# First unit of an attention kernel: row turns one slot later, modulation ahead of the first turn, second x tile loaded early

## The chip, the cores and the metric

The kernel runs on one core of a Trainium2 chip. Its time is device microseconds of a whole run; the span in a profile is from the first to the last instruction of one profiled run. The engines are named as in the profile: PE is TensorE (PEld its weight loads), DVE VectorE, ACT ScalarE, POOL GpSimd, SP the engine that issues most loads. All times inside a run are microseconds from the start of its span.

## The reference, cut to what matters

```python
mod = silu(c) @ w_mod                      # six rows of 512: sa, ca, ga, sb, cb, gb
h = layernorm(x) * (1 + ca) + sa           # x: 2048 x 512
q = h @ wq                                 # 32 heads of 128; k, v caches: 8 groups, 2048 keys
p = softmax(q k^T / sqrt(128));  o = p v
x = x + ga * (o @ wo)
# then a gated MLP over the same rows, with a 2048 x 2048 spatial product
```

The argument concerns only the first 35 us: how the first four row tiles (128 rows each) of `x` become queries while the first scores are already being computed.

## The kernel before

A *unit* is one group of four heads and one row tile; it has eight *slots*. Slot i of unit u computes scores for 256 keys (`qk`, two matmuls of 512 columns, then one exponential of 1024 columns on ScalarE), and the values (`pv`) of unit u - 1. `fill` is work put at the end of a slot, `at` work put at its start. `bank2()` gives one of two score buffers `s_ps`, `bank("misc")` one of two other PSUM banks. TensorE executes its matmuls in exactly this program order. A *turn* transposes the normalised rows of one row tile on TensorE and then scales and shifts them by `ca` and `sa` (four *modulations* on VectorE). The *projection* makes queries of the turned tile. `warm(n)` is n idle matmuls on zeros. `mod_part` computes the columns of `sa` or `ca` with 16 matmuls of one column; where the text says "the modulation" in one word, it means the second such set, `ca`.

```python
# loads, all on SP (cut): w_mod first and second half, wq in two parts, then
load_k_nat(0)
load_k_nat(1)
nc.sync.dma_start(out=x_sb[:, 1:CT, :], in_=x_dram[:, 1:CT, :])     # row tiles 1 to 3
# (x tile 0 comes on the ScalarE queue)
...
xns0 = ln1_norm(0, 1, ln1_stats(0, 1))
mc_ps = bank("misc")
warm(10)
mod_part(0, wmod_a, 0, mc_ps)          # 16 matmuls of one column: sa
warm(6)
x_ps = [...]
for dt in range(NDT):                  # first turn: transpose row tile 0
    nc.tensor.transpose(x_ps[dt % 2][...], xns0[0][...], ident[:])
mod_part(1, wmod_a, D, mc_ps)          # 16 matmuls: ca
mod_copy(0, mc_ps)
warm(2)
...                                    # modulate, project tile 0, first scores
def first_norm():                      # at the end of slot 0
    k_turn((4, 5, 6, 7), (nc.vector.tensor_copy,))
    ln_stats(mv1, 2, x_sb[:, 2, :])
    first["x1"] = ln1_norm(1, 1, first["r1"])
    ln_stats(mv1, 3, x_sb[:, 3, :])
    first["r2"] = rstd_of(mv1[:, 2:4, :], 2, "ln1")

def first_turn():
    ln1_turn(1, 1, first["x1"])        # 4 transposes, then 4 modulations on VectorE
    first["x2"] = ln1_norm(2, 2, first["r2"])

at(0, 2, first_turn)
at(0, 5, lambda: ln1_turn(2, 2, first["x2"]))
fill[0, 0] = [first_norm]
for i in (1, 2, 4):
    fill[0, i] = [lambda: warm(1)]     # one idle matmul
fill[0, 3] = qproj(0, list(range(REP)), P, P)                 # 16 matmuls, tile 1
rest_q = qproj(0, [0, 1], 2 * P, 2 * P) + qproj(0, [2, 3], 2 * P, 2 * P)
fill[0, 6], fill[0, 7], fill[1, 0] = rest_q[0:5], rest_q[5:11], rest_q[11:16]
```

`ln1_turn` puts its four blocks into two banks, two blocks in each:

```python
for half in range(2):
    t_ps = bank("misc")[:].bitcast(BF16).rearrange("p (k q) -> p k q", k=2)
    ...                                # transposes of blocks 2*half, 2*half+1, then their modulation
```

Of the kernel before, what the change touches and what calls it, by code (L numbers as in the profile page):

```python
# [15 lines left out]
P = 128  # L16
# [559 lines left out]
def kernel(  # L576
# [19 lines left out]
    nc = tc.nc  # L596
    _, S, D = A_x.shape
    _, HKV, SK, DH = A_k_cache.shape
    HQ = A_wq.shape[1] // DH
    REP = HQ // HKV  # L600
# [9 lines left out]
    CT = 512 // P  # L610
# [7 lines left out]
    x_dram = A_x[0].rearrange("(t p) d -> p t d", p=P)  # L618
# [27 lines left out]
    x_sb = res.tile([P, NT, D], BF16, name="x_sb")  # L646
# [9 lines left out]
    wmod_a = res.tile([P, NDT, 2 * D], BF16, name="wmod_a")  # L656
# [6 lines left out]
    def bank(name):  # L663
        return psum.tile([P, 512], FP32, name=name)

    def bank2():
        return psum.tile([P, 1024], FP32, name="s_ps")
# [35 lines left out]
    def load_k_nat(half):  # L703
        t0, t1 = half * NKT // 4, (half + 1) * NKT // 4
        nc.sync.dma_start(
            out=k_nat[:, t0 * P : t1 * P].rearrange("p (t d) -> p t d", d=DH),
            in_=k_rows[:, t0:t1, :],
        )
# [35 lines left out]
    for dts in (slice(0, 2), slice(2, 4)):  # L744
        nc.sync.dma_start(out=wqs[0][:, dts, :], in_=wq_dram[:, dts, 0 : REP * DH])  # L745
    load_k_nat(0)
    load_k_nat(1)
    nc.sync.dma_start(out=x_sb[:, 1:CT, :], in_=x_dram[:, 1:CT, :])

    kT0 = early.tile([P, SK], BF16, name="kT")  # L750
    groups[0] = dict(kT=kT0)
# [23 lines left out]
    def warm(n):  # L775

        w_ps = bank("o_ps")
        for k in range(n):
            nc.tensor.matmul(
                w_ps[:].rearrange("p (r d) -> p r d", r=REP),  # L780
                lhsT=zeros[:, 0, :],
                rhs=zeros[:],
                start=True,
                stop=True,
            )


    def ln1_stats(j0, n):
        for j in range(j0, j0 + n):
            ln_stats(mv1, j, x_sb[:, j, :])  # L790
        return rstd_of(mv1[:, j0 : j0 + n, :], n, "ln1")
# [9 lines left out]
    def hT_of(ch):  # L801
        if ch not in hTs:
            hTs[ch] = res.tile([P, NDT, 512], BF16, name="hT", bufs=NCH)
        return hTs[ch]

    def ln1_mod(dst, src, dt):
        nc.vector.tensor_scalar(
            out=dst,
            in0=src,
            scalar1=modc[:, NDT + dt : NDT + dt + 1],  # L810
            scalar2=modc[:, dt : dt + 1],
            op0=ALU.mult,
            op1=ALU.add,
        )

    def ln1_turn(j0, n, xns):

        ch, c0 = j0 // CT, (j0 % CT) * P
        hT = hT_of(ch)
        for half in range(2):  # L820
            t_ps = bank("misc")[:].bitcast(BF16).rearrange("p (k q) -> p k q", k=2)
            for k in range(2):
                dt = half * 2 + k
                for jj in range(n):
                    nc.tensor.transpose(
                        t_ps[:, k, jj * P : (jj + 1) * P],
                        xns[jj][:, dt * P : (dt + 1) * P],
                        ident[:],
                    )
            for k in range(2):  # L830
                dt = half * 2 + k
                dst, src = hT[:, dt, c0 : c0 + n * P], t_ps[:, k, 0 : n * P]
                ln1_mod(dst, src, dt)
# [10 lines left out]
    def mod_part(i, wmod, w0, mc_ps):  # L844

        for dt in range(NDT):
            for kt in range(NDT):
                nc.tensor.matmul(
                    mc_ps[:, i * NDT + dt : i * NDT + dt + 1],
                    lhsT=wmod[:, kt, w0 + dt * P : w0 + (dt + 1) * P],  # L850
                    rhs=sc_bf[:, kt : kt + 1],
                    start=(kt == 0),
                    stop=(kt == NDT - 1),
                )

    def mod_copy(first, mc_ps):
        c0 = first * NDT
        nc.vector.tensor_copy(out=modc[:, c0 : c0 + NDT], in_=mc_ps[:, 0:NDT])
        nc.vector.tensor_scalar_add(
            out=modc[:, c0 + NDT : c0 + 2 * NDT], in0=mc_ps[:, NDT : 2 * NDT], scalar1=1.0  # L860
        )
# [15 lines left out]
    mc_ps = bank("misc")  # L877
    warm(10)
    mod_part(0, wmod_a, 0, mc_ps)
    warm(6)  # L880

    x_ps = [bank("misc")[:].bitcast(BF16), bank2()[:, 0:512].bitcast(BF16)]
    for dt in range(NDT):
# [2 lines left out]
            xns0[0][:, dt * P : (dt + 1) * P],  # L886
            ident[:],
        )
    mod_part(1, wmod_a, D, mc_ps)
    mod_copy(0, mc_ps)  # L890
    warm(2)
    hT_of(0)
    for k in range(2):
        for dt in (2 * k, 2 * k + 1):
# [3 lines left out]
            else:  # L898
                nc.scalar.activation(
                    out=dst,  # L900
                    in_=src,
# [17 lines left out]
    for hf, copy in enumerate((nc.vector.tensor_copy, nc.scalar.copy)):  # L919
        copy(  # L920
            out=qTs[0][:, 2 * hf : 2 * hf + 2, 0:P],
            in_=q_ps[hf][:, 0 : 2 * P].rearrange("p (h q) -> p h q", h=2),
# [3 lines left out]
    def qproj(b, heads, c0, n):  # L926

        g, ch = divmod(b, NCH)
        if b not in qTs:
            qTs[b] = early.tile([P, REP, 512], BF16, name="qT")  # L930
        one = n * len(heads) <= 512
        ps = {}

        def mm(hh, dt):
            if dt == 0 and (not one or hh == heads[0]):
                ps[0] = bank("misc")
            o0 = (hh - heads[0]) * n if one else 0
            nc.tensor.matmul(  # L938
                ps[0][:, o0 : o0 + n],
                lhsT=wqs[g][:, dt, hh * DH : (hh + 1) * DH],  # L940
                rhs=hTs[ch][:, dt, c0 : c0 + n],
                start=(dt == 0),
                stop=(dt == NDT - 1),
            )
            if dt == NDT - 1 and (not one or hh == heads[-1]):
                hs = heads if one else [hh]
                dst = qTs[b][:, hs[0] : hs[-1] + 1, c0 : c0 + n]
                src = ps[0][:, 0 : len(hs) * n].rearrange("p (h q) -> p h q", q=n)
                nc.vector.tensor_copy(out=dst, in_=src)  # L949

        return [lambda hh=hh, dt=dt: mm(hh, dt) for hh in heads for dt in range(NDT)]

    first = dict(r1=ln1_stats(1, 1))
# [6 lines left out]
    def at(it, slot, fn):  # L960
        later.setdefault((it, slot), []).append(fn)
# [156 lines left out]
    fill = {}  # L1118
# [8 lines left out]
        ln1_turn(1, 1, first["x1"])  # L1127
        first["x2"] = ln1_norm(2, 2, first["r2"])

    at(0, 2, first_turn)  # L1130
    at(0, 5, lambda: ln1_turn(2, 2, first["x2"]))
    fill[0, 0] = [first_norm]
    for i in (1, 2, 4):
        fill[0, i] = [lambda: warm(1)]
    fill[0, 3] = qproj(0, list(range(REP)), P, P)
    rest_q = qproj(0, [0, 1], 2 * P, 2 * P) + qproj(0, [2, 3], 2 * P, 2 * P)
    fill[0, 6], fill[0, 7], fill[1, 0] = rest_q[0:5], rest_q[5:11], rest_q[11:16]

    def ln1_at(ch, stats, norm, turn):
        st = {}  # L1140
# [169 lines left out]
    for f in range(NFT):  # L1310
# [6 lines left out]
        out=ok1[:], in0=rall[:], scalar1=1.0 / SAFE, scalar2=None, op0=ALU.is_ge  # L1317
# [8 lines left out]
        out=bad[:], in0=okm[:], scalar1=-1.0, scalar2=1.0, op0=ALU.mult, op1=ALU.add  # L1326
# [137 lines left out]
```

## Time and profile before

| | before |
|---|---|
| median of six runs | 1323.25 us (1322.82 to 1323.65) |
| span of the profiled run | 1321.5 us |
| first score matmul | 10.63 |
| slot 2's scores of unit 0 | 13.38 |
| slot 2's scores of unit 1 | 21.94 |
| fifth reciprocal of the values (unit 2) | 40.91 |

The prediction shows the lines that carry the argument; to them belong two lines of TensorE's timeline around the first turn, and one of unit 1. The columns of a timeline are start, duration, engine, line, operation, output and inputs, shapes, count, and in brackets the idle time before it and who ended it.

```profile
7.27 0.22 PE L884 MATMUL s_ps<-ident,xn 128*128 128x128 bf16 x1
7.45 0.55 PE L848 MATMUL misc<-sc_bf,wmod_a 128*128 128x1 bf16 x16
...
21.94 0.59 PE L971 MATMUL s_ps<-qT,kT 128*128 128x512 bf16 x2
```

The last block of the first turn runs at 7.27 and the second set of modulation matmuls behind it, as soon as its weights have landed (7.4).

### The profile page before, as it was taken

To read this page: it belongs to the slowest core of one execution; us is meant where nothing else is said; L and a number is where in the kernel's file an instruction comes from. 1 tells how busy PE (TensorE), PEld (TensorE's weight loads), DVE (VectorE), ACT (ScalarE), POOL (GpSimd) and SP (SyncE) were. 2 spreads that over 40 slices of the span, in tenths; PEclk is the share of its full clock that TensorE was granted. 3 is DMA by queue.
4 is the path that set the end of the run, shared out by engine and by line. 5 is a ranking of instruction groups with operands and counts; after the bars stand their busy time and mean duration, and the time that the engine had idled before them with its cause. 6 is when DMAs were issued, how large, how long until landed. Compare 5 with 4: busy or idle time off the path is not lost.

```text
span 1321.5 us, 27879 instructions
## 1 busy us (share of the span) xinstructions
PE 1312.4 (99%) x12335; PEld 858.3 (65%) x12335; DVE 473.5 (36%) x1166; ACT 1077.8 (82%) x1061; POOL 49.4 (4%) x92
## 2 busy tenths in 40 slices
PE   9999999999999999999999999999999999999998
PEld 5666666666666666666666666666666666644445
DVE  5632222222222222222222222222222566794444
ACT  6898999999999999999999999999999999650000
POOL 1200000000000000000000000000000000120000
PEclk9999999999999999999999999999999999999999
DMA  7541022102111112111110211021101111143300
GB/s 180 141 104 33 14 49 37 37 15 51 31 23 35 32 37 37 31 35 37 33 36 14 53 37 33 18 53 21 33 14 21 25 33 30 33 116 80 69 21 26
DMA packets 148704, 58.12 MB, mean 44 GB/s; under 512 B 138368, under 2 KB 144768, under 8 KB 148576
## 3 DMA queue, kind: packets, MB, share of 16 engines
q1 hardware_dynamic: 141776, 37.65, 15.1%
q0 software_dynamic: 4208, 16.39, 4.1%
q10 hardware_dynamic: 2592, 2.23, 0.5%
q8 instruction: 98, 1.61, 0.5%
q14 instruction: 30, 0.25, 0.1%
HBM read 21.37 MB, written 2.10 MB: 18 GB/s over the span
## 4 chain that ended last, share of the span: by engine, by line
PE 98%; DMA 0%; DVE 0%; SPq 0%; issue 0%
PE o_ps L993 35%; PE s_ps L971 33%; PE misc L1025 8%; PE misc L938 8%; PE misc L1344 7%; PE s_ps L1190 2%; PE s_ps L1229 2%; PE o_ps L1365 1%; PE s_ps L1365 1%; DMA x_sb<-in_A_x_dram 0%; PE misc L1101 0%; DVE tmp L1377 0%; DVE yout L1378 0%; DVE bnst L691 0%; SPq L700 0%; SPq L745 0%
## 5 line engine op out<-in xcount | busy, mean ns | idle before, releaser
L978 ACT ACTIVATE pT<-s_ps 128x1024 bf16<-128x1024 f32 x1024 | 1044.5, 1025 | 82.9 <-PE s_ps L971 9.0
L993 PEld LDWEIGHTS <-pT 128*128 128x128 bf16 x8192 | 548.5, 98 | 241.2
L993 PE MATMUL o_ps<-v,pT 128*128 128x129 bf16 x8192 | 631.4, 220 | 0.0
L971 PE MATMUL s_ps<-qT,kT 128*128 128x512 bf16 x2048 | 609.0, 379 | 0.0
L1004 DVE RECIPROCAL rall<-o_ps 128x2 f32<-128x2 f32 x256 | 43.7, 171 | 743.8 <-PE o_ps L993 743.5
L971 PEld LDWEIGHTS <-kT 128*128 128x128 bf16 x2048 | 199.3, 98 | 118.7 <-DVE qT L920 0.5
L1025 PE MATMUL misc<-wo_g,oT 128*128 128x512 bf16 x512 | 194.0, 379 | 0.0
L938 PE MATMUL misc<-hT,wq_g 128*128 128x512 bf16 (+2 forms) x528 | 189.6, 371 | 0.0
L1005 DVE TENSOR_TENSOR onorm<-o_ps,rall 128x256 bf16<-128x256 f32 x256 | 108.7, 425 | 9.0 <-DVE rall L1004 0.3
L1344 PE MATMUL misc<-wsp,z 128*128 128x512 bf16 (+2 forms) x560 | 100.7, 336 | 0.0
L949 DVE CAST qT<-misc 128x512 bf16<-128x512 f32 x127 | 86.3, 681 | 1.8 <-PE misc L938 1.6
L1344 PEld LDWEIGHTS <-z 128*128 128x128 bf16 x560 | 50.6, 98 | 48.5
L1038 DVE TENSOR_TENSOR xacc<-misc,xacc 128x512 f32<-128x512 f32 x112 | 76.2, 680 | 0.0
L938 PEld LDWEIGHTS <-wq_g 128*128 128x128 bf16 x528 | 50.6, 98 | 1.1 <-issue 0.2
L1025 PEld LDWEIGHTS <-oT 128*128 128x128 bf16 x512 | 50.1, 98 | 0.8
L1359 DVE TENSOR_TENSOR gb<-misc,bsp_bc 128x512 bf16<-128x512 f32 (+1 forms) x28 | 18.4, 659 | 59.0 <-PE misc L1344 59.0
L1190 PE MATMUL s_ps<-win_sb,hT 128*128 128x448 bf16 x128 | 27.0, 352 | 0.0
L1200 ACT ACTIVATE z<-s_ps 128x896 bf16<-128x896 f32 x16 | 14.7, 917 | 14.9 <-PE s_ps L1190 14.9
L1229 PE MATMUL s_ps<-hT,win_sb 128*128 128x512 bf16 x112 | 24.5, 379 | 0.0
L1237 ACT ACTIVATE z1T<-s_ps 128x1024 bf16<-128x1024 f32 x14 | 14.3, 1024 | 10.0 <-PE s_ps L1229 9.1
L691 DVE BATCH_NORM_STATS2 bnst<-x_sb 128x6 f32<-128x512 bf16 x32 | 21.9, 684 | 1.5 <-DMA x_sb<-in_A_x_dram 1.0
L715 POOL DMA_DIRECT2D wq_g<-in_A_wq_dram x7 | 5.3, 753 | 420.9 <-PE misc L938 420.9
(87 smaller groups left out, 283.2 us busy)
## 6 DMA issues: line engine op xcount, KB each, us to landing
wq_g<-in_A_wq_dram POOLq DMA_DIRECT2D x7, 512.0 KB, 3.8
v<-in_A_v_cache_dram POOLq DMA_DIRECT2D x7, 512.0 KB, 7.2
wo_g<-in_A_wo_dram POOLq DMA_DIRECT2D x7, 512.0 KB, 4.7
oT<-onorm SPq DMA_TRANSPOSE x128, 2.4
wsp<-in_w_mod_dram POOLq DMA_DIRECT2D x1, 2048.0 KB, 11.7
out_dram<-yout ACTq DMA_DIRECT2D x16, 128.0 KB, 1.7
win_sb<-in_B_w_in_dram POOLq DMA_DIRECT2D x1, 1792.0 KB, 7.7
x_sb<-in_A_x_dram SPq DMA_DIRECT2D x3, 512.0 KB, 5.6
```

The costliest lines, as they stand in the source:

```text
L938: nc.tensor.matmul(ps[0][:, o0 : o0 + n], lhsT=wqs[g][:, dt, hh * DH : (hh + 1) * DH], rhs=hTs[ch][:, dt, c0 : c0 + n], start=(dt == 0), s ...
L949: nc.vector.tensor_copy(out=dst, in_=src)
L971: nc.tensor.matmul(s_ps[:, h * 512 : (h + 1) * 512].rearrange("p (r q) -> p r q", r=REP), lhsT=groups[g]["kT"][:, kt * P : (kt + 1) * P], ...
L978: nc.scalar.activation(out=pTs[u][:, 2 * i : 2 * i + 2, :], in_=s_ps[:].rearrange("p (k q) -> p k q", k=2), func=ACT.Exp, scale=inv_sqrt_dh,)
L993: nc.tensor.matmul(o_ps[:, hh % 2, 0 : DH + 1], lhsT=pTs[u][:, kt, hh * P : (hh + 1) * P], rhs=groups[g]["v1"][:, kt, 0 : DH + 1], start=( ...
L1004: nc.vector.reciprocal(out=rall[:, c0 : c0 + 2], in_=o_ps[:, :, DH])
L1005: nc.vector.tensor_tensor(out=onorms[u][:, hh - 1 : hh + 1, :], in0=o_ps[:, :, 0:DH], in1=rall[:, c0 : c0 + 2].unsqueeze(2).to_broadcast([ ...
L1025: nc.tensor.matmul(X_ps[:], lhsT=oTs[u][:, hh, :], rhs=groups[g]["wo"][:, hh, :], start=(hh == 0), stop=(hh == REP - 1),)
L1038: nc.vector.tensor_tensor(out=xaccs[j][:], in0=X_ps[:], in1=xaccs[j][:], op=ALU.add)
L1190: nc.tensor.matmul(ps[0][:, hf * 512 : hf * 512 + FC], lhsT=h2Ts[j // CT][:, dt, (j % CT) * P : (j % CT + 1) * P], rhs=win_sb[:, dt, FH + ...
L1229: nc.tensor.matmul(ps[0][:, k * 512 : (k + 1) * 512], lhsT=win_sb[:, dt, f * P : (f + 1) * P], rhs=h2Ts[2 * ch2 + k][:, dt, :], start=(dt ...
L1344: nc.tensor.matmul(g_ps[:, :n], lhsT=z2[:, st, f * P : (f + 1) * P], rhs=wsp[t][:, st, c0 : c0 + n], start=(st == 0), stop=(st == NT - 1 a ...
```

## The change

Its intent: take the wait for the second tile's normalised rows out of TensorE's queue by putting the turn behind one more slot of scores, and bring forward what the first turns need.

```diff
     load_k_nat(0)
+    nc.sync.dma_start(out=x_sb[:, 1, :], in_=x_dram[:, 1, :])
     load_k_nat(1)
-    nc.sync.dma_start(out=x_sb[:, 1:CT, :], in_=x_dram[:, 1:CT, :])
+    nc.sync.dma_start(out=x_sb[:, 2:CT, :], in_=x_dram[:, 2:CT, :])
 ...
     warm(6)
+    mod_part(1, wmod_a, D, mc_ps)
 ...                                    # first turn
-    mod_part(1, wmod_a, D, mc_ps)
     mod_copy(0, mc_ps)
 ...
-    at(0, 2, first_turn)
-    at(0, 5, lambda: ln1_turn(2, 2, first["x2"]))
+    at(0, 3, first_turn)
+    at(0, 6, lambda: ln1_turn(2, 2, first["x2"]))
     fill[0, 0] = [first_norm]
-    for i in (1, 2, 4):
+    for i in (1, 2, 3):
         fill[0, i] = [lambda: warm(1)]
-    fill[0, 3] = qproj(0, list(range(REP)), P, P)
+    fill[0, 4] = qproj(0, list(range(REP)), P, P)
 ...
-    fill[0, 6], fill[0, 7], fill[1, 0] = rest_q[0:5], rest_q[5:11], rest_q[11:16]
+    fill[0, 7], fill[1, 0], fill[1, 1] = rest_q[0:5], rest_q[5:11], rest_q[11:16]
```

As in the prediction, the modulation's new place is (a), the load (b), the later slots (c).

## The prediction

> **What bounds the kernel now.** I read the page first: its chain of waits, then its groups.
>
> ```profile
> PE 98%; DMA 0%; DVE 0%; SPq 0%; issue 0%
> L978 ACT ACTIVATE pT<-s_ps 128x1024 bf16<-128x1024 f32 x1024 | 1044.5, 1025 | 82.9 <-PE s_ps L971 9.0
> ```
>
> The chain that ended last is TensorE for 98% of 1321.5 us. ScalarE's exponentials fill 1044.5 us and wait only 9.0 us for scores. So only a microsecond that TensorE idles, or is held back by the exponentials, can be won. Next I read who waited for whom, TensorE alone, whole span; it is the whole list:
>
> ```profile
> PE o_ps L779 <- DVE onorm L761: 1.2, 1, 1.2
> PE misc L825 <- DVE xn L680: 1.1, 1, 1.1
> PE misc L848 <- DMA wmod_a<-in_w_mod_dram: 0.4, 1, 0.4
> PE misc L912 <- DVE hT L807: 0.3, 1, 0.3
> PE s_ps L1365 <- DVE yT L1360: 0.3, 1, 0.3
> ```
>
> These waits sum to 3.3 us, 0.25% of the span. The second is the change's target. The timeline of the first 26 us, one engine at a time, shows it:
>
> ```profile
> 11.71 0.38 PE L779 MATMUL o_ps<-onorm 128*128 128x512 bf16 x1
> 13.15 0.40 PE L825 MATMUL misc<-ident,xn 128*128 128x128 bf16 x4 [1.05 <-DVE xn L680]
> 13.38 0.59 PE L971 MATMUL s_ps<-qT,kT 128*128 128x512 bf16 x2
> ...
> 14.46 1.37 PE L938 MATMUL misc<-hT,wq_g 128*128 128x128 bf16 x16
> ...
> 12.70 0.39 DVE L680 TENSOR_SCALAR xn<-x_sb,mv,rstd_ln 128x512 bf16<-128x512 bf16 x1
> 13.01 0.69 DVE L691 BATCH_NORM_STATS2 bnst<-x_sb 128x6 f32<-128x512 bf16 x1
> 13.73 0.18 DVE L692 BATCH_NORM_AGGREGATE mv<-bnst 128x2 f32<-128x6 f32 x1
> 13.83 1.07 DVE L807 TENSOR_SCALAR hT<-misc,modc 128x128 bf16<-128x128 bf16 x4
> ...
> 11.26 1.94 ACT L978 ACTIVATE pT<-s_ps 128x1024 bf16<-128x1024 f32 x2 [0.68 <-PE s_ps L971]
> 14.01 1.94 ACT L978 ACTIVATE pT<-s_ps 128x1024 bf16<-128x1024 f32 x2 [0.81 <-PE s_ps L971]
> 16.30 4.98 ACT L978 ACTIVATE pT<-s_ps 128x1024 bf16<-128x1024 f32 x5 [0.35 <-PE s_ps L971]
> ```
>
> The reader is to see three things. The turn of the second row tile (L825) stands in program order ahead of slot 2's scores, and its normalised rows exist only at 13.09, so the queue stands still behind it. ScalarE then starves 0.81 us. And the projection of that tile (L938, 14.46) waits inside itself for the four modulations on VectorE, which end at 14.90.
>
> **What the Trainium skill says.** "TensorE: Matmul & The Clock Gate", Part 2, Step-by-step: only weight loads are pulled ahead; "The MATMULs themselves stay in program order". The trace agrees: slot 2's scores need nothing from the turn, yet run 0.23 us after it, at 13.38. The same page, Part 1, puts 512 columns at about 216 ns back to back; the chain lists pairs of score matmuls at 0.43 us. "DMA: Bandwidth & Descriptors", Anatomy of one DMA, says of the software path that a fixed part of some 2 us is mostly the receipt of the last write; these loads are of the hardware path. Of it the trace shows that landings trail the bytes: by the GB/s of 1 us windows some 1.18 MB (the first x tile and both modulation halves) had moved by 6.1 us, while the second half landed at 1.48 + 5.9 = 7.38.
>
> **The change part by part.** No instruction is added or removed except one more DMA issue; the warming matmuls stay three (slots 1, 2, 3 in place of 1, 2, 4).
>
> (a) Modulation columns ahead of the first turn: 16 small matmuls, 7.45 to about 7.86. They can't start before 7.38, where their weights land; today the four transposes (7.09) run in that gap. Afterwards TensorE waits some 0.3 us, then does the columns, then transposes at 7.87 to 8.1. The column copies on VectorE keep 8.04 to 8.27 and the first modulation 8.30; it needs a transpose done by about 8.1. The query projection begins at 8.79, and its weight load was put down to a DMA:
>
> ```profile
> PEld L912 <- DMA wq_g<-in_A_wq_dram: 0.8, 1, 0.8
> ```
>
> The second half of these weights lands at 2.76 + 6.0 = 8.76. So this part is worth 0, within 0.1 either way.
>
> (b) The second x tile ahead of the second part of k. Its statistics started at 10.75, having waited 0.23 us for the 384 KB load (4.35 + 6.4 = 10.75). Alone it is 128 KB, and at the 370 GB/s of 8 to 9 us lands some 0.7 us ahead of the other two tiles and 0.4 ahead of where the k part was: about 9.7. VectorE is free at 10.52 after its copy of the first queries, so the statistics start 0.2 earlier. But the k copy behind them still waits for TensorE's transposes (11.06 plus 0.39), and the next tile's statistics follow it, so normalised rows come only 0.08 earlier, at about 13.0. The second k part lands at 3.87 + 5.8 + 0.4, about 10.1, against a need at 11.06: hidden. The transposing load of the other half of k moves by up to 0.5 to about 12.2, against slot 4 (15.67): hidden.
>
> (c) Turns and projections one slot later. I re-ran the queue by hand with the durations above: scores 0.43 a slot, a warming matmul 0.21, turn 0.22 (four), projection of the second tile 0.0685 a matmul (13 in 0.89), later projections 0.109 a matmul, values 0.45 a slot; exponentials 1.02 long at a pitch of 0.92 (11.26 to 12.18). Scores of slot n wait for exponential n-2, as s_ps has two buffers.
>
> - Slot 2 scores: exponential 0 ends 12.28, so 12.30 to 12.73, against 13.38.
> - A warming matmul to 12.94; turn waits for rows, 13.07 to 13.29.
> - Slot 3 scores to 13.72, warming to 13.93; slot 4 scores wait for exponential 2 (13.10 to 14.12): 14.14 to 14.57. Before, slot 4 came only after the projection, at 15.84.
> - Projection: three matmuls, then the fourth modulation (now 14.82), then 13 x 0.0685 = 0.89: ends 15.76 (before: 15.84). It stays pinned by VectorE, but slot 4 is already behind it.
> - Slot 5 to 16.19; second turn 16.19 to 16.72 (its second half waits for the copy of the queries); slot 6 to 17.15; slot 7 waits for exponential 5 (16.39 to 17.41): 17.43 to 17.86.
> - Unit 1: the last projections now lie at the ends of slot 7, slot 0 and slot 1: 5, 6 and 5 matmuls of 0.109. With scores and values this brings slot 2 of unit 1 to 21.38, against 22.11 before.
>
> So TensorE gains 22.11 - 21.38 = 0.73 us: of the 1.23 us hole (11.92 to 13.15) 0.5 us is given back as three short waits, for exponential 0, for the rows and for exponentials 2 and 5.
>
> (d) ScalarE's cut. From here exponentials bind: a slot of scores and values takes 0.885 us on TensorE (scores start at 22.83, 23.71, 24.60), an exponential 12.02/13 = 0.925. Before, the unbroken row of exponentials began at 21.69 with slot 1 of unit 1, so slot 2's at 22.61. Afterwards slot 2's starts when its scores are out, 21.38 + 0.60 = 21.98. That is 0.63 earlier, carried on until 32.8, where projections make TensorE the bound again, and from there to the end. I take this smaller figure.
>
> Sum: 0 + 0.63 (the 0.08 of (b) is inside it). 1323.28 - 0.63 = 1322.65, which I state as 1322.6.
>
> **Rivals.** *The wait only moves.* The projection's end hardly moves (15.84 to 15.76), and a later turn could become the new hole. For it: VectorE is busy 4.47 of 5 us between 10 and 15. Against: slots now stand ahead of it, with ready scores to do. If slot 4's scores find no free buffer before the modulations are out, only 0.1 to 0.3 us is left: about 1323.0.
>
> *ScalarE becomes the bound and takes it all.* Between 25 and 32.8 it already is, so an early lead of TensorE is worthless unless ScalarE has it too. It gets it here, since the idle times of 0.81 and 0.35 close. If late projections in slots 0 and 1 of unit 1 starve it again, the gain falls to 0.3: 1323.0.
>
> *The start moves later.* If modulation waits beyond 7.45, or the transposes behind it hold up the first rows, everything shifts by up to 0.3: 1322.9 to 1323.3, no gain. Against: a DMA at 8.76 is the floor there anyway.
>
> *More than I count.* If the first queries were held by the first turn rather than by weights, the head wins another 0.3 to 0.5: 1322.2.
>
> **Range and chances.** The three runs before spread over 0.41 us. With that and the rivals, 8 in 10 lie between 1321.9 and 1323.3. A 2% change needs 26 us; all TensorE waits together are 3.3 us, and nothing steady is touched. So faster by over 2%: 0.005; slower: 0.005; within: 0.99.
>
> **What would show it.** In the changed profile: the wait of L825 for xn falls from 1.1 us to under 0.3; slot 2's scores run about 12.3, before the turn; the third exponential starts near 13.1, not 14.01; the projection still ends near 15.8; slot 2 of unit 1 starts near 21.4; the first row of score matmuls stays at 10.63 within 0.1; the modulation columns still start at 7.4, now with a TensorE wait on their DMA of some 0.3 us. The prediction is wrong if the first scores move by more than 0.2 us, if the late projections in unit 1 delay the transposed loads of the next rows past their use at 32.8 (the modulations there waited 2.87 us for their DMA, until 31.01; the first two are out at about 31.7, 1.1 us ahead of the first projections, and 0.5 us would be left), or if a later stage that waits on time rather than on TensorE swallows the lead.

## The result, and the profile after

| | before | changed |
|---|---|---|
| median, six runs each | 1323.25 us | 1322.38 us (1322.12 to 1322.57) |
| span of the profiled run | 1321.5 us | 1320.8 us |
| first score matmul | 10.63 | 10.65 |
| slot 2's scores of unit 0 | 13.38 | 12.35 |
| slot 2's scores of unit 1 | 21.94 | 21.46 |
| fifth reciprocal of the values | 40.91 | 40.40 |

The medians differ by 0.87 us. The ratio is 0.9994, interval 0.9981 to 1.0006: the same within 2%. The slowest of the six runs after (1322.57) is below the fastest of the six before (1322.82), so the direction is plain, the size less so.

First, all waits of TensorE in the changed kernel. The columns are engine, waiting tile and line, whom it waited for, us in total, times, longest. Lines of this kernel stand one or two higher than before: L825 is now L826, L848 is L849.

```profile
PE o_ps L780 <- DVE onorm L762: 1.2, 1, 1.2
PE misc L849 <- DMA wmod_a<-in_w_mod_dram: 0.6, 2, 0.4
PE s_ps L1366 <- DVE yT L1361: 0.3, 1, 0.3
PE misc L1345 <- issue: 0.3, 2, 0.2
PE misc L913 <- DVE hT L808: 0.3, 1, 0.3
PE s_ps L972 <- ACT pT L979: 0.2, 1, 0.2
```

The wait of the turn for its rows, 1.1 us before, is off the list (0.11 us is left, too short for it). Two shorter ones stand in its place: slot 2's scores for exponential 0 (0.2), and the modulation for its weights (0.6 in two waits, 0.4 in one before). The row of L1345 is no wait: it stands in the lists of the nine traces that miss matmul records (below), and in none of the other five. Next the timelines of TensorE, VectorE and ScalarE, in that order:

```profile
11.73 0.38 PE L780 MATMUL o_ps<-onorm 128*128 128x512 bf16 x1
12.35 0.59 PE L972 MATMUL s_ps<-qT,kT 128*128 128x512 bf16 x2 [0.24 <-ACT pT L979]
12.78 0.38 PE L780 MATMUL o_ps<-onorm 128*128 128x512 bf16 x1
13.10 0.40 PE L826 MATMUL misc<-ident,xn 128*128 128x128 bf16 x4
...
14.61 1.17 PE L939 MATMUL misc<-hT,wq_g 128*128 128x128 bf16 x16
...
21.46 0.59 PE L972 MATMUL s_ps<-qT,kT 128*128 128x512 bf16 x2
...
12.66 0.38 DVE L680 TENSOR_SCALAR xn<-x_sb,mv,rstd_ln 128x512 bf16<-128x512 bf16 x1
...
11.28 4.69 ACT L979 ACTIVATE pT<-s_ps 128x1024 bf16<-128x1024 f32 x5 [0.68 <-PE s_ps L972]
16.25 4.02 ACT L979 ACTIVATE pT<-s_ps 128x1024 bf16<-128x1024 f32 x4 [0.29 <-PE s_ps L972]
20.66 1.02 ACT L979 ACTIVATE pT<-s_ps 128x1024 bf16<-128x1024 f32 x1 [0.39 <-PE s_ps L972]
22.09 4.69 ACT L979 ACTIVATE pT<-s_ps 128x1024 bf16<-128x1024 f32 x5 [0.41 <-PE s_ps L972]
```

Slot 2's scores now run before the turn, at 12.35. ScalarE does five exponentials in a row where it did two, stopped 0.81 us and did two. The stop before 16.25 was there before (0.35, before 16.30). In unit 1 it stops twice, before 20.66 and 22.09, where it stopped once (0.41, before 21.69): the late projections now end two of unit 1's slots instead of one, and keep scores from it.

One row of the page misleads. Before and changed:

```profile
PE 1312.4 (99%) x12335; PEld 858.3 (65%) x12335; DVE 473.5 (36%) x1166; ACT 1077.8 (82%) x1061; POOL 49.4 (4%) x92
PE 1301.5 (99%) x12130; PEld 858.3 (65%) x12335; DVE 473.4 (36%) x1166; ACT 1076.7 (82%) x1061; POOL 49.2 (4%) x92
```

TensorE's busy time falls by 10.9 us in a kernel that is 0.7 us shorter. Nothing was saved: 205 matmul records are missing (12130 of 12335), while all 12335 weight loads are there with the same busy time. The Trainium skill, "Perfetto Trace Analysis", Identifying the Most-Contended Engine, calls matmul busy time a poor measure of how near a kernel is to the hardware's peak, and weight-load busy time a better one; these two rows agree, although the reason here is missing records, not the pipelining that the page gives.

To compare traces I use VectorE's 256 reciprocals of the values, one for each half unit. From the fifth on they run at the same distance in both kernels: 0.51 us earlier at 40.91, and still 0.51 at the last (1145.80 to 1145.29). The last VectorE instruction ends 0.51 earlier too (1317.28 to 1316.77). From there to the end of the span it is about 4.2 us before and 4.0 after, and 3.8 to 4.2 over all 14 profiles. So the change acts in the first 41 us alone, and some tenths of a microsecond of any single time are the end's.

### The profile page after: what moved, and what is told of

It reads as the page before. It is cut to its first block, busy times and chain, and to the rows that moved or that the text cites. A ratio compares the mean times of both kernels' runs of the same rounds, so it can differ in the third digit from the quotient of the medians. Undisturbed runs are those within 1.5% of the kernel's fastest.

```text
span 1320.8 us, 27675 instructions
## 1 busy us (share of the span) xinstructions
PE 1301.5 (99%) x12130; PEld 858.3 (65%) x12335; DVE 473.4 (36%) x1166; ACT 1076.7 (82%) x1061; POOL 49.2 (4%) x92
## 4 chain that ended last, share of the span: by engine, by line
PE 98%; issue 1%; DMA 0%; DVE 0%; ACT 0%; SPq 0%; DVEq 0%
PE s_ps L972 36%; PE o_ps L994 35%; PE misc L939 7%; PE misc L1345 7%; PE misc L1026 6%; PE s_ps L1191 2%; PE s_ps L1230 2%; PE o_ps L1366 1%; PE s_ps L1366 0%; DMA wmod_a<-in_w_mod_dram 0%; PE misc L1102 0%; DVE tmp L1378 0%; DVE yout L1379 0%; PE misc L849 0%; PE misc L1353 0%
## 5 line engine op out<-in xcount | busy, mean ns | idle before, releaser
L939 PE MATMUL misc<-hT,wq_g 128*128 128x512 bf16 (+2 forms) x466 | 166.4, 370 | 0.1
L1026 PE MATMUL misc<-wo_g,oT 128*128 128x512 bf16 x386 | 146.3, 379 | 0.0
L1345 PE MATMUL misc<-wsp,z 128*128 128x512 bf16 (+2 forms) x555 | 100.5, 336 | 0.6 <-issue 0.3
L1345 PEld LDWEIGHTS <-z 128*128 128x128 bf16 x560 | 50.6, 98 | 48.5
```

The lines of the kernel that those rows point to most:

```text
L939: nc.tensor.matmul(ps[0][:, o0 : o0 + n], lhsT=wqs[g][:, dt, hh * DH : (hh + 1) * DH], rhs=hTs[ch][:, dt, c0 : c0 + n], start=(dt == 0), s ...
L1026: nc.tensor.matmul(X_ps[:], lhsT=oTs[u][:, hh, :], rhs=groups[g]["wo"][:, hh, :], start=(hh == 0), stop=(hh == REP - 1),)
L1345: nc.tensor.matmul(g_ps[:, :n], lhsT=z2[:, st, f * P : (f + 1) * P], rhs=wsp[t][:, st, c0 : c0 + n], start=(st == 0), stop=(st == NT - 1 a ...
```

## The experiments

With the kernel before and the changed one, twelve kernels ran on the chip, two of them twice, all correct. Two readings are taken from each trace: when the first score matmul starts (what the *head* costs), and the *stretch* from there to the fifth reciprocal (what the slots cost). Before: 10.63 and 40.91 - 10.63 = 30.28. The last column is the median minus that of the kernel before in the same rounds.

| run | what it is | first scores | stretch | median, us | minus before |
|---|---|---|---|---|---|
| before | | 10.63 | 30.28 | 1323.25 | |
| changed | (a), (b), (c) | 10.65 | 29.75 | 1322.38 | -0.87 |
| c_only | (c) | 10.69 | 29.75 | 1322.70 | -0.39 |
| ab_only | (a), (b) | 10.62 | 30.21 | 1322.90 | -0.19 |
| no_a | (b), (c) | 10.79 | 29.75 | 1322.88 | -0.21 |
| no_b | (a), (c) | 10.42 | 29.86 | 1322.91 | -0.18 |
| dbl_new | changed, tile 0 normalised twice | 10.51 | 29.75 | 1322.37 | -0.77 |
| dbl_old | no_a, tile 0 normalised twice | 10.85 | 29.75 | 1322.78 | -0.36 |
| slot4 | turn in slot 4 | 10.59 | 29.90 | 1322.77 | -0.37 |
| slot1 | turn in slot 1 | 10.95 | 30.74 | 1323.48 | +0.34 |
| after2 | changed, again | 10.32 | 29.75 | 1322.53 | -0.55 |
| no_a2 | no_a, again | 10.49 | 29.75 | 1322.52 | -0.56 |
| onebank | changed, turns in one bank | 10.83 | 29.60 | 1322.28 | -0.80 |
| onebank_spread | and last projections spread | 10.33 | 29.50 | 1322.16 | -0.92 |

How to read it: the stretch repeats to 0.01 us in seven traces of five programs that differ only ahead of it (the eighth, no_b, gave 29.86; why is said below), the first scores do not: identical programs gave 10.65 and 10.32 (changed, after2), 10.79 and 10.49 (no_a, no_a2). The 30.28 rests on one trace of the kernel before. The timed medians scatter by some tenths: the changed kernel gave -0.87 and -0.55. The record lists three chips (c_only to no_b on one, the dbl runs and slots on another, the rest on a third), so the last column is safest within such a group; the changed kernel was not run again in the first two. So parts of (c) are settled by the stretch, and parts that act on the head need care.

### Each part alone and left out

c_only keeps the loads and the modulation as before, with this and only this edit:

```diff
-    at(0, 2, first_turn)
-    at(0, 5, lambda: ln1_turn(2, 2, first["x2"]))
+    at(0, 3, first_turn)
+    at(0, 6, lambda: ln1_turn(2, 2, first["x2"]))
     # warm(1) in slots 1, 2, 3; qproj at (0, 4); rest_q at (0, 7), (1, 0), (1, 1)
```

> Part (c) alone: turns and projections one slot later, loads and modulation as before. 'Lead' is how much earlier than in the kernel before the reciprocals of the values run in the trace, from the second on (27.51 us before); the changed kernel leads by 0.51 us. Theory (the turn's slot carries it): the normalised rows come at 13.09 as before, the turn starts at 13.15, slot 2's scores at 12.3, lead 0.45 (0.40 to 0.50), since only the 0.05 us that (b) gave the rows is missing; first scores at 10.63. Rival (the loads or the modulation carry it): lead under 0.15.

It led by 0.47 (40.44), 0.53 when counted from the first scores: all of the stretch's gain. Counted from the first scores the rows were even as early as in the changed kernel (2.01 us after them in both), since tile 1 had landed before VectorE was free.

ab_only takes the changed kernel and puts the turns back into slots 2 and 5, the projections into slots 3, 6, 7 and 0.

> Parts (a) and (b) without (c): modulation ahead of the first turn and the second x tile loaded early, turns where they were. Theory: the second turn still stands ahead of slot 2's scores and waits for rows that come 0.05 us earlier; lead 0.05 (0 to 0.10), TensorE's wait for xn still about 1.0 us. Rival (loads or modulation carry it): lead 0.3 to 0.5.

It led by 0.08, and TensorE's wait for the rows is back. From its timeline:

```profile
13.07 0.40 PE L826 MATMUL misc<-ident,xn 128*128 128x128 bf16 x4 [0.99 <-DVE xn L680]
```

So the turn's slot carries the stretch, and the rival is out. no_a and no_b are the changed kernel with one part put back:

```diff
 # no_a
     warm(6)
-    mod_part(1, wmod_a, D, mc_ps)
 ...                                    # first turn
+    mod_part(1, wmod_a, D, mc_ps)
     mod_copy(0, mc_ps)
 # no_b
     load_k_nat(0)
-    nc.sync.dma_start(out=x_sb[:, 1, :], in_=x_dram[:, 1, :])
     load_k_nat(1)
-    nc.sync.dma_start(out=x_sb[:, 2:CT, :], in_=x_dram[:, 2:CT, :])
+    nc.sync.dma_start(out=x_sb[:, 1:CT, :], in_=x_dram[:, 1:CT, :])
```

> The change without the early load of the second x tile. Theory: statistics of tile 1 start at 10.75 again, not 10.46, but the rows come only 0.05 us later (13.09), lead 0.45 (0.40 to 0.50). Rival (the early load is what lets the turn move): the turn waits again, 0.3 us or more beyond the 0.11 of the changed kernel, lead under 0.25.

no_b's head came early (10.42), so VectorE caught up with the load and waited 0.28 us for tile 1; the stretch was 29.86. In c_only the same load order cost nothing. So (b) is worth 0 to 0.11 us, depending on which of the two is early. The lead of 0.63 in this trace lies outside the expected 0.40 to 0.50 because the head moved, not the slots. The traced run took 1322.43 us; three of no_b's five took 1322.91 to 1323.08, so what (b) is worth in those is not shown.

> The change without the modulation ahead of the turn. Theory: (a) is worth nothing, because its weights land at 7.38 and the query weights at 8.76: first scores at 10.63 instead of 10.65, lead 0.51 to 0.53. Rival (the head gains by it): lead under 0.40 and first scores later than 10.65.

This one went against my theory: the lead was 0.37 and the first scores ran at 10.79, which is what the rival had said. The stretch, 29.75, is untouched, so it is the head. TensorE's timeline of no_a shows where, and under it that of ab_only, in which the first x tile landed as late (its rows were normalised from 7.02 and 6.99; 6.62 in the profile before):

```profile
7.49 0.23 PE L885 MATMUL misc<-ident,xn 128*128 128x128 bf16 x1
...
7.72 0.54 PE L849 MATMUL misc<-sc_bf,wmod_a 128*128 128x1 bf16 x16
```

```profile
7.44 0.54 PE L849 MATMUL misc<-sc_bf,wmod_a 128*128 128x1 bf16 x16
7.85 0.22 PE L886 MATMUL misc<-ident,xn 128*128 128x128 bf16 x1
```

In the old order the modulation stands behind the turn, and the turn waits for the rows; when the rows are late, so is everything behind it. In the new order it starts at 7.44 all the same. The pair is not clean: the modulation's weights landed at about 7.1 in ab_only and at about 7.5 in no_a, so the new order could have saved no_a only some 0.2 us. And one trace each could be chance, since loads land differently in each run. Hence the next pair.

### Making the first rows late on purpose

```diff
-    xns0 = ln1_norm(0, 1, ln1_stats(0, 1))
+    r0 = ln1_stats(0, 1)
+    xns0 = ln1_norm(0, 1, r0)
+    normalise(xns0[0][:], x_sb[:, 0, :], mv1[:, 0, 0:1], r0[:, 0:1])
```

The same values are written a second time, which takes VectorE 0.45 us while it has nothing else to do. dbl_new is the changed kernel with this edit, dbl_old is no_a with it.

> The changed kernel, with the first x tile normalised twice (the same values written again): its rows are ready some 0.4 us later, as if the tile had landed late. Theory (modulation ahead of the turn is an insurance: the modulation is pinned by its own weights at about 7.4 and no longer stands behind the turn): TensorE's second 16 modulation matmuls still start at about 7.45, the turn follows at about 7.9, first scores 10.65, not later than 10.75. Rival (the order of the two doesn't matter, the head is pinned by the query weights): the same here and in the run beside it.

> The changed kernel without the modulation ahead of the turn, and with the first tile normalised twice. Theory: the turn waits for the rows until about 7.45 (until 7.85 where the tile lands late besides), and the modulation, the column copies and the first query projection stand behind it: first scores 10.85 to 11.25, so 0.2 to 0.5 us later than in the run beside it, and the reciprocals of the values as much later. Rival: first scores 10.65 to 10.75, as there.

From TensorE's timelines, the first dbl_new, the second dbl_old:

```profile
7.33 0.55 PE L849 MATMUL misc<-sc_bf,wmod_a 128*128 128x1 bf16 x16
7.74 0.22 PE L888 MATMUL misc<-ident,xn 128*128 128x128 bf16 x1
...
10.51 0.59 PE L974 MATMUL s_ps<-qT,kT 128*128 128x512 bf16 x2
```

```profile
7.55 0.23 PE L887 MATMUL misc<-ident,xn 128*128 128x128 bf16 x1 [0.20 <-DVE xn L680]
...
7.78 0.54 PE L849 MATMUL misc<-sc_bf,wmod_a 128*128 128x1 bf16 x16
...
10.85 0.59 PE L974 MATMUL s_ps<-qT,kT 128*128 128x512 bf16 x2
```

The rows were late in both; only the old order passed it on: first scores 0.34 us later, the fifth reciprocal 0.34 (40.60 against 40.26), the median of five 0.41 (1322.22 to 1322.49 against 1322.63 to 1323.08). The changed kernel doesn't notice the doubled work (1322.37 against its own 1322.38 and 1322.53). What the doubling costs the old order in time is not shown: dbl_old (-0.36) lies between no_a (-0.21) and no_a2 (-0.56).

The 14 traces together show what sets the head. In each of them the first query projection starts 1.31 to 1.35 us after the second set of modulation matmuls: no_b 7.17 and 8.49, after2 7.25 and 8.56, before 7.45 and 8.79, changed 7.47 and 8.80, no_a 7.72 and 9.06, dbl_old 7.78 and 9.12. Between the two lie the column copies and the first modulations. The second half of the query weights does not set it: in dbl_old it had landed at 2.76 + 5.9, about 8.7, 0.4 before that projection. From the projection to the first scores it is 1.73 to 1.93 us more (2.34 in slot1), longer where the first k load comes late. So the mechanism of (a) is shown: it takes the modulation, from which the head runs on, out from behind a load that varies. What it is worth without help was tried once more:

> The changed kernel without the modulation ahead of the turn, again. Theory (the modulation's place saves 0.1 to 0.3 us in the runs in which the first x tile lands late, nothing in the others): median 0.1 to 0.4 above the control of the same call. If the tile lands early in this trace (its rows from 6.6), first scores at 10.6; if late (from 6.9), at 10.7 to 10.85. Rival (that difference was chance): median within 0.1 of the control.

> The changed kernel again, as a control beside the next three: 1322.4 us (1322.1 to 1322.7), 0.7 to 0.9 below the kernel before; from first scores to the fifth reciprocal of the values 29.75 us, as in its first trace; first scores between 10.4 and 10.65 unless a load is late.

Here the medians are equal (1322.52 and 1322.53), the means 0.15 apart, and the heads 0.17 (10.49 and 10.32). In no_a2 the modulation stood behind the turn until 7.42, although its weights had landed at 1.48 + 5.6 = 7.08. So the order in the trace is as the theory says, but the first scores (10.49) came earlier than either expected time, and the expected 0.1 to 0.4 of median is not there. The worth of (a) in plain runs stays open between 0 and about 0.3 us; timed runs that scatter by 0.5 don't settle it.

### One slot more, two slots fewer

```diff
 # slot4
-    at(0, 3, first_turn)
-    at(0, 6, lambda: ln1_turn(2, 2, first["x2"]))
+    at(0, 4, first_turn)
+    at(0, 7, lambda: ln1_turn(2, 2, first["x2"]))
     # qproj at (0, 5); rest_q at (1, 0), (1, 1), (1, 2)
 # slot1: first_turn at (0, 1), second turn at (0, 4), qproj at (0, 2),
 #        warm(1) in 1, 3, 4, rest_q at (0, 5), (0, 6), (0, 7)
```

> The changed kernel with turns and projections one more slot later (turn in slot 4, projection in slot 5, second turn in slot 7, the last projections in slots 0, 1 and 2 of unit 1). From first scores to the fifth reciprocal of the values it is 30.28 us before and 29.75 changed. Theory (each step trades a wait for rows against a wait for exponentials, and the rows' wait is all but gone at slot 3: 0.11 us): nothing more to win, slot 5's scores wait for exponential 3 (about 0.5 us) and the late projections starve ScalarE in unit 1: 30.2 (30.0 to 30.4), the gain given back. Rival (every slot later gives TensorE as much again): 29.3 or less.

> The changed kernel with turns and projections two slots earlier (turn in slot 1, projection in slot 2, second turn in slot 4, last projections in slots 5 to 7). Theory (the turn in program order holds the scores behind it): TensorE waits for the rows from 11.3 to 13.1, 1.6 to 1.8 us, and one slot of scores more, 0.43 us, stands behind it: from first scores to the fifth reciprocal 30.7 (30.5 to 30.9) against 30.28 before. Rival (TensorE's wait costs nothing because ScalarE or VectorE set the pace here): 30.1 to 30.3.

```profile
PE misc L826 <- DVE xn L680: 1.6, 1, 1.6
```

slot1 waited 1.6 us (the line is from its list of waits) and its stretch is 30.74, as expected; its late head, 10.95, is a k load that came 0.4 us late, not the turn. slot4's direction was right, its size wrong: 29.90, only 0.15 worse than the changed kernel, where I had expected 0.45. Slot 5's scores do wait for exponential 3 as foreseen (0.33 us in TensorE's timeline, at 15.04), but the slots behind made up most of it. So over slots 1, 2, 3, 4 the stretch is 30.74, 30.21, 29.75, 29.90: slot 3 is the best of the four.

### What is left: two variants

In the changed kernel the second turn took from 16.05 to 16.79, though its eight transposes need about 0.44: its second half waits for the bank that still holds the queries. onebank puts a turn into one bank:

```diff
-        for half in range(2):
-            t_ps = bank("misc")[:].bitcast(BF16).rearrange("p (k q) -> p k q", k=2)
-            ...
+        t_ps = bank("misc")[:].bitcast(BF16).rearrange("p (k q) -> p k q", k=NDT)
+        for dt in range(NDT):          # all transposes into t_ps[:, dt], then all modulations
```

> The changed kernel, with each turn's four blocks in one bank of PSUM instead of two. In the changed kernel the second turn's second half (16.55) waits for the bank that the copy of the queries frees at 16.48, so TensorE loses 0.3 us between 16.05 and 16.79. Theory (TensorE's short waits in unit 0 are what is left, and ScalarE follows): slot 6's scores, exponential 6 and the first scores of unit 1 come 0.25 earlier; from first scores to the fifth reciprocal 29.53 (29.45 to 29.62) instead of 29.75, and the time some 0.2 below the control. Rival (the next wait, for exponential 5 or for the second turn's modulations, takes its place): 29.70 to 29.80.

onebank_spread adds

```diff
-    fill[0, 7], fill[1, 0], fill[1, 1] = rest_q[0:5], rest_q[5:11], rest_q[11:16]
+    fill[0, 7], fill[1, 0] = rest_q[0:5], rest_q[5:8]
+    # and two each at (1, 1), (1, 2), (1, 3), (1, 4)
```

> The last run's kernel with the last eleven projections of the first unit spread over slots 0 to 4 of unit 1 (3, 2, 2, 2, 2) instead of slots 0 and 1 (6, 5). Theory (ScalarE's idle times of 0.39 and 0.41 us ahead of the exponentials of slots 1 and 2 of unit 1 cost, since exponentials bind from there): these shrink, exponentials are unbroken from slot 3 or 4 on and 0.13 earlier; 29.40 (29.30 to 29.50). Rival (TensorE's work alone counts, and its sum is the same): as in the last run, within 0.03.

The second turn of onebank and the slots behind it, from TensorE's timeline; under it the exponentials of onebank_spread from ScalarE's:

```profile
16.24 0.61 PE L824 MATMUL misc<-ident,xn 128*128 128x128 bf16 x8
16.68 0.59 PE L969 MATMUL s_ps<-qT,kT 128*128 128x512 bf16 x2
17.51 0.59 PE L969 MATMUL s_ps<-qT,kT 128*128 128x512 bf16 x2 [0.23 <-ACT pT L976]
```

```profile
19.86 12.77 ACT L976 ACTIVATE pT<-s_ps 128x1024 bf16<-128x1024 f32 x13 [0.16 <-PE s_ps L969]
```

The turn's wait is gone (16.24 to 16.68), and slot 7 waits for exponential 5 instead. 29.60 lies in the expected range; 0.15 of the 0.3 is kept, the rest became that wait. Spreading the projections closes ScalarE's stops (13 exponentials in a row from 19.86) and gains another 0.10, less than the 0.13 hoped for and at the edge of the range, but not the rival's 0.03. The head of onebank (10.83) is late for another reason than in no_a: the six idle matmuls ahead of the second modulation took 2.05 us in its trace (1.46 to 1.60 in the others), so the modulation started at 7.78, 0.5 after its weights had landed. The traced run is the slowest of onebank's five (1322.8). The medians, 1322.28 and 1322.16, are below the changed kernel's 1322.53 of the same rounds. onebank_spread is the fastest kernel here, with the shortest stretch; a difference of 0.25 us in the stretch is sure, in the time it is within the scatter of single runs.

## Why the prediction was right

The time, 1322.38 (1322.53 again), lies in the range, near 1322.6. By its steps:

- **Bound.** Right. Apart from missing records, only TensorE's waits in the first 25 us moved, and the lead stays the same to the end of the span.
- **(a), "worth 0, within 0.1 either way".** This is the step that failed, in its reason and in its size. The reason was a floor, the query weights landing at 8.76. The head has another: the projection follows the second modulation by 1.31 to 1.35 us in all 14 traces, and that modulation is what (a) moves. The size came from one trace whose rows were early (6.62), so that its modulation stood behind nothing (7.45 against weights at 7.38). In the two traces of the old order in which they came late by themselves (c_only, no_a) it started at 7.62 and 7.72, and with the rows late on purpose the old order's head was 0.34 us later than the new one's, its median 0.41 higher. The foreseen wait for the modulation's weights (0.3) is there: 0.38 at 7.47 in the changed kernel's timeline.
- **(b), rows "only 0.08 earlier".** Rows from 12.66 instead of 12.70, 0.04. In the traces 0 to 0.11 all told.
- **(c), TensorE's 0.73.** Measured 21.94 - 21.46 = 0.48. Most of the miss is a wrong "before": slot 2's scores of unit 1 ran at 21.94 there, not 22.11, so the hand run's 21.38 meant 0.56. Slot 2 at 12.35 (12.30 said), turn 13.10 (13.07), slot 4 14.18 (14.14), slot 5 behind the projection 15.62 (15.76), slot 2 of unit 1 21.46 (21.38). The projection did wait for its fourth modulation, 0.12 us, to 14.90; but the 13 matmuls from there took 0.72 us, not 0.89. The prediction had counted to the modelled end of the last one (15.84), while slot 4's scores ran from 15.67 before. The second turn gave this back: its second half waited until 16.57, and it ended at 16.79, not 16.72; slot 0 of unit 1 started at 18.50, not 18.41.
- **(d), ScalarE's cut to 0.63.** There is no cut. The exponential of slot 2 of unit 1 leads by 0.52 (22.61 to 22.09), its scores by 0.48. The smaller figure that the prediction took was the larger one, once 22.11 is put right. The exponential started at 22.09, not 21.98. Of the 0.11, 0.08 is TensorE's later scores, 0.03 the time from scores to exponential (0.63 instead of 0.60).
- **Rivals.** "The wait only moves" is right for some of it: 0.24 us for exponential 0, and ScalarE's stops in unit 1, which the last variant then recovered in part. "The start moves later" did not happen in this trace. The test that went with it, wrong if the first scores move by more than 0.2 us, assumes a head that repeats: the same kernel's second trace (10.32) would have failed it.
- **A reading.** That landings trail the bytes is not shown: the 1.18 MB are of all loads together, and the query weights were issued from 2.13 on. Nothing in the sum rests on it.

So the sum came out well partly by luck: the slots gave 0.53 where 0.63 was said, and (a), counted as nothing, can add up to about 0.3. The timed gain was 0.87 in six runs and 0.55 in five; how much of what lies beyond 0.53 is (a)'s is not shown.

## What to carry to other kernels

In an engine that works in program order, put work whose input arrives late behind work whose input is there, and move it back slot by slot until its wait is gone. One slot further (slot4) scores waited 0.33 us for an exponential, and the stretch grew by 0.15. A wait that a trace doesn't show can still be there in other runs, when two loads race: order the queue so that the work that a variable load holds up has nothing independent behind it. Where the gain is far below the scatter of times, measure a stretch inside the traces, which here repeated to 0.01 us.

## What the Trainium skill lacked or had wrong

- "DMA: Bandwidth & Descriptors", Latency and other measured facts, gives fixed and loaded latencies, but no spread from run to run. Here the first x tile let VectorE's first statistics start between 4.69 and 5.09 (4.71 to 5.09 in four runs on one chip), and in one and the same program (changed and after2, perhaps on different chips) the second half of the modulation's weights landed at about 7.4 and 6.9.
- None of the pages that I read says that a trace can miss matmul records and that weight-load records are then the check: 12130 matmuls against 12335 weight loads, and 10.9 us of TensorE busy time that nobody saved.
- "TensorE: Matmul & The Clock Gate" states that matmuls stay in program order, which these runs confirm (0.99 and 1.6 us of ready scores held behind a turn); it doesn't say what that costs, or that the remedy is an order of issue with a best point (stretch 30.74, 30.21, 29.75, 29.90 for the turn in slots 1 to 4).
